# Block orders of the moving reads in a Strassen matmul kernel: 4 words against 16 and 4 by turns, and 512 columns in pieces

## The chip, the cores and the metric

The kernel runs on one core of one Trainium2 chip. The metric is the device time of one execution in microseconds (us); lower is better.

## What is computed

The reference joins an attention block and a two-layer network with softplus. All inputs are float32.

```python
# q, k, v: (8, 8, 576, 64); g_norm: (64,)
kv  = einsum('bhsd,bhse->bhde', k, v)
out = einsum('bhsd,bhde->bhse', q, kv)
rms = sqrt(mean(out * out, axis=-1, keepdims=True) + 1e-06)
x   = (out / rms * g_norm)          # then (B,H,S,D) -> (B*S, H*D) = (4608, 512)
h   = x @ w_in                      # w_in (512, 2048)
g   = maximum(h, 0) + log1p(exp(-abs(h)))
y   = g @ w_out                     # w_out (2048, 512), y (4608, 512)
```

## The kernel before

The precision comes from splitting. Each float32 factor is written as pieces of type float32r (the fast matmul type for 4-byte words), and each product is the sum of three matmuls over `m`, all added up in one PSUM bank.

The work has three phases. In phase 0 the attention part runs (L696 and L720 are its matmuls, L738 and L776 its transposes), and for a first share of the hidden columns the network runs on blocks of 384 tokens: L863 multiplies x by w_in (12 matmuls of 384 columns each time), L870 multiplies the softplus result by w_out (512 columns, three matmuls for each group of 128 tokens).

Phases 1 and 2 take the rest of the hidden columns, in pairs of 128-column chunks and on 512 tokens at a time. They form x times w_in by Strassen's scheme, seven products in place of eight: `wide_step` adds the tasks of one such step. Each product is a call of `product(u, q)`: six matmuls at L1065, `m` from 0 to 2 and in it `kd` from 0 to 1 (two halves of 128 rows of the contraction), all with 256 moving columns, all added up in a quarter of a two-bank PSUM tile that `place(q)` gives. The moving operand is a unit of x (tiles `units`, `early`, `turned`), the stationary one a form of w_in (tiles `pieces`, `w`, `half`). ScalarE and VectorE copy and add between the products (L1107 to L1115), apply softplus, and split the result into `gv` and `g` (L1123, L1126, L1129). Then `mm2(c, i)` multiplies by w_out: three matmuls at L1136, of 512 moving columns each, added up in one PSUM bank for each of four groups of 128 tokens. There the moving operand is `outs[c]`, a tile of `pieces`. In all there are 2,016 matmuls at L1065 and 1,152 at L1136.

The order of the work is not found at run time. A planner (`Plan`) is given each task with a fixed cost and a position, simulates the engines, and writes one static order for each engine's queue, PE's included. Its costs are constants in the code (710 ns for a product, 700 for one `mm2`), so its order does not depend on how an operand is addressed.

The kernel already reads the 256-column operands in an order of its own. `from_the_end` cuts a row into blocks of 4 words and takes the blocks from the last to the first; the words in a block stay in order. Applied to the moving operand and to the PSUM output alike it changes the order in which columns pass, not where they land:

```python
def from_the_end(x):
    return x.rearrange("p (b w) -> p b w", w=4)[:, ::-1]
```

The 512-column matmuls of L1136, and those of L863 and L870, read and write plainly from the first word to the last.

Of the kernel before, what the change touches and what calls it, by code (L numbers as in the profile page):

```python
# [9 lines left out]
F32R = mybir.dt.float32r  # L10
# [8 lines left out]
P = 128  # L19
# [19 lines left out]
    return x.rearrange(f"r ({' '.join(names)}) -> r {' '.join(names)}", **dict(zip(names, shape[1:])))  # L39


def from_the_end(x):

    return x.rearrange("p (b w) -> p b w", w=4)[:, ::-1]


class Slot:
# [159 lines left out]
def kernel(  # L207
# [24 lines left out]
    nc = tc.nc  # L232
# [810 lines left out]
    def wide_step(k):  # L1043
        ph, n, p = STEPS[k]
        ab, gv = slot("ab"), slot("gvp")
        b = starts[k]
# [3 lines left out]
        mine = list(wide_sums)  # L1050
        outs = [w_slots[1, c] for c in (2 * p, 2 * p + 1)]

        def place(q):
            return ab.tile[:, q // 2, q % 2 * HW:(q % 2 + 1) * HW]
# [3 lines left out]
        def product(u, q):  # L1058
            f, i = PRODUCTS[u]
            w = forms[p][f].tile  # L1060
            dst, v = unit_slots[ph, n, u]
            for m in range(3):
                for kd in range(2):
                    at = i * 2 * P + kd * P
                    nc.tensor.matmul(from_the_end(place(q)), lhsT=w[:, m, at:at + P],  # L1065
                                     rhs=from_the_end(dst.tile[:, m, v, kd] if u < 6 else dst.tile[:, m, kd]),
                                     start=(u == 0 and not m and not kd), stop=(m == 2 and kd == 1), skip_group_check=True)

        def multiply(u, q, after, pos, take=(), follows=None):
            f = PRODUCTS[u][0]  # L1070
            give = [unit_slots[ph, n, u][0]] if last else []
            if final and u in (2, 3, 5, 6):
                give.append(forms[p][f])
            return add("PE", 710, lambda: product(u, q), unit_done[ph, n, u] + forms_done[p][f] + list(after), pos, take, give,
                       follows=follows)
# [3 lines left out]
        def gt(dtype=F32):  # L1079
            if dtype not in held:  # L1080
                held[dtype] = sb.tile([P, 2, WIDE], dtype, tag=f"g{gv.place}", name=f"g{gv.place}_{dtype == F32}")
            return held[dtype]

        def gvt(m, dtype=F32):
            y = gv.tile[:, m]
            return y if dtype == F32R else y.bitcast(F32)
# [8 lines left out]
        def begin():  # L1095
            new(ab, None)
            product(0, X)
# [33 lines left out]
        def mm2(c, i):  # L1131
            fresh = first and not c and ph < LAST
            if fresh:
                new(mine[i], [P, d_model])
            for m in range(3):
                nc.tensor.matmul(mine[i].tile, lhsT=(gvt(m, F32R) if m < 2 else gt(F32R))[:, c, i * P:(i + 1) * P], rhs=outs[c].tile[:, m],  # L1136
                                 start=fresh and not m, stop=(last and c == 1 and m == 2), skip_group_check=True)

        seeds = {}
# [19 lines left out]
        for c in range(2):  # L1159
            for i in range(TW):  # L1160
                slot_pos = b + PACE + MM2[TW * c + i]
                a2 = add("PE", 700, lambda c=c, i=i: mm2(c, i),
                         [split_done[c]] + factors_done[1, 2 * p + c] + ([seeds[i]] if i in seeds and not c else []) +
                         ([before[i]] if c or not first else []), slot_pos, [mine[i]] if first and not c and ph < LAST else [], [gv] + ([outs[c]] if final else []))
                before[i] = a2
                if last and c:
                    leave(ph, TW * n + i, mine[i], a2, slot_pos)
# [98 lines left out]
```

## Time and profile before

| | |
|---|---|
| median of 3 runs | 865.46 us (864.7 to 867.28) |
| the profiled execution | 864.34 us, span 862.5 us |
| mean granted TensorE clock | 0.999 |
| PE, PEld busy | 849.7 and 757.7 us (99% and 88%) |
| DVE, ACT busy | 704.6 and 521.2 us (82% and 60%) |
| first L1065 matmul, last matmul start | 338.5 us, 858.4 us |

PE is the matmul unit, PEld its weight loads, which run beside it; DVE is VectorE, ACT is ScalarE. The span goes from the first instruction to the last, the execution's time has some 2 us more around it. The matmuls are pipelined: the duration of one in the trace (282 ns in the mean at L1065, some 390 at L1136) includes the way through the array, and the next starts long before it ends. What counts for the total is the time from one start to the next, and it is read from the start column of the timeline.

### The profile page before, as it was taken

The numbers are of one execution on the slowest core, as the hardware profiler recorded it, in microseconds if no ns is written. First come the engines' busy times: TensorE is split into PE (matmuls) and PEld (weight loads), VectorE is DVE, ScalarE is ACT, GpSimd is POOL, SyncE is SP. The second block draws the span as 40 slices with busy tenths as digits, with TensorE's granted clock in tenths as the row PEclk, the third lists the DMA queues.
The fourth block names the chain that finished last, engine by engine and source line by source line (L and its number), as shares of the span: only waits on it lengthen the run. The fifth ranks groups of instructions, "written<-read, shape, count | busy, mean of one in ns | idle before, by whom it ended". The sixth has DMA issues, their size and how long they took to land.

```text
span 862.5 us, 17080 instructions
## 1 busy us (share of the span) xinstructions
PE 849.7 (99%) x6464; PEld 757.7 (88%) x6464; DVE 704.6 (82%) x995; ACT 521.2 (60%) x980; POOL 76.1 (9%) x79
## 2 busy tenths in 40 slices
PE   8899999999999999999999999999999999999998
PEld 5578888898888999999999999998999899999996
DVE  7988898888788888798888788878788766788873
ACT  6866664436354467766667665654868555566654
POOL 0342223111113300000000000000000000000000
PEclk9999999999999999999999999999999999999999
DMA  9998997779784655436645546645364753778863
GB/s 285 283 234 222 261 263 242 178 235 226 210 188 118 188 157 183 141 107 216 199 158 164 166 154 205 190 158 176 123 196 138 232 165 102 244 234 240 247 187 130
DMA packets 239778, 167.07 MB, mean 194 GB/s; under 512 B 106320, under 2 KB 198736, under 8 KB 239696
## 3 DMA queue, kind: packets, MB, share of 16 engines
q1 hardware_dynamic: 239392, 165.86, 65.7%
q8 instruction: 50, 0.82, 0.4%
q14 instruction: 32, 0.26, 0.1%
q10 hardware_dynamic: 304, 0.13, 0.1%
HBM read 112.98 MB, written 52.95 MB: 192 GB/s over the span
## 4 chain that ended last, share of the span: by engine, by line
PE 94%; DVE 1%; ACT 1%; POOL 0%; issue 0%; ACTq 0%; DVEq 0%
PE banks L1136 30%; PE banks L1065 28%; PE banks L870 16%; PE banks L863 15%; PE banks L720 2%; PE banks L696 2%; PE banks L738 0%; DVE units L643 0%; DVE half L732 0%; PE banks L1230 0%; POOL roots L728 0%; DVE units L646 0%; DVE roots L724 0%; DVE m L464 0%; ACT units L640 0%
## 5 line engine op out<-in xcount | busy, mean ns | idle before, releaser
L1136 PE MATMUL banks<-pieces,gv 128*128 128x512 f32 x768 | 238.0, 391 | 0.0
L1136 PE MATMUL banks<-pieces,g_False 128*128 128x512 f32 x384 | 149.4, 389 | 0.0
L1136 PEld LDWEIGHTS banks<-pieces,gv 128*128 128x128 f32 x768 | 132.5, 188 | 17.3
L863 PE MATMUL banks<-units,pieces 128*128 128x384 f32 x768 | 145.4, 337 | 0.0
L870 PE MATMUL banks<-pieces,gv 128*128 128x512 f32 x576 | 144.9, 396 | 0.0
L863 PEld LDWEIGHTS banks<-units,pieces 128*128 128x128 f32 x768 | 135.5, 188 | 4.9
L870 PEld LDWEIGHTS banks<-pieces,gv 128*128 128x128 f32 x576 | 106.1, 188 | 20.3
L1065 PEld LDWEIGHTS banks<-units,pieces 128*128 128x128 f32 x840 | 112.0, 188 | 6.5 <-ACT banks L1111 0.4
L1065 PE MATMUL banks<-units,pieces 128*128 128x256 f32 x840 | 116.4, 282 | 0.0
L885 ACT ACTIVATE half<-banks 128x384 f32<-128x384 f32 x64 | 31.5, 492 | 97.3 <-PE banks L863 97.1
L1126 DVE TENSOR_TENSOR gv<-g_True,gv 128x1024 fp32r<-128x1024 f32 x47 | 57.5, 1224 | 36.5 <-ACT gv L1123 36.5
L1136 PEld LDWEIGHTS banks<-pieces,g_False 128*128 128x128 f32 x384 | 72.1, 188 | 15.7
L1065 PEld LDWEIGHTS banks<-units,w 128*128 128x128 f32 x504 | 67.3, 188 | 3.7 <-ACT banks L1111 0.2
L1065 PE MATMUL banks<-units,w 128*128 128x256 f32 x504 | 70.3, 282 | 0.0
L728 POOL TENSOR_TENSOR roots<-roots,half 128x8 f32<-128x8 f32 x36 | 62.2, 1727 | 3.0
L1129 DVE SCALAR_TENSOR_TENSOR g_False<-gv 128x1024 fp32r<-128x1024 f32 x47 | 57.6, 1225 | 1.5
L1028 DVE TENSOR_TENSOR units<-loads,units 128x1024 fp32r<-128x1024 f32 x42 | 51.2, 1219 | 6.2 <-ACT units L1025 6.1
L1093 ACT ACTIVATE g_True<-banks 128x256 f32<-128x256 f32 x96 | 36.7, 383 | 31.6 <-PE banks L1065 31.0
L1115 DVE TENSOR_TENSOR g_True<-banks,g_True 128x512 f32<-128x512 f32 x48 | 33.2, 691 | 27.7 <-PE banks L1065 22.5
L930 ACT ACTIVATE m<-banks 128x512 f32<-128x512 f32 x72 | 42.1, 595 | 18.7 <-PE banks L1136 12.8
L1031 DVE SCALAR_TENSOR_TENSOR units<-units 128x1024 fp32r<-128x1024 f32 x42 | 51.4, 1224 | 1.8
L1025 ACT ACTIVATE units<-loads 128x1024 fp32r<-128x1024 f32 x42 | 44.5, 1059 | 12.4 <-PE banks L1065 8.9
(115 smaller groups left out, 1250.2 us busy)
## 6 DMA issues: line engine op xcount, KB each, us to landing
loads<-x SPq DMA_DIRECT2D x180, 128.0 KB, 2.7
part<-m SPq DMA_DIRECT2D x72, 256.0 KB, 2.9
m<-part SPq DMA_DIRECT2D x72, 256.0 KB, 3.3
loads<-form SPq DMA_DIRECT2D x45, 256.0 KB, 3.3
form<-loads SPq DMA_DIRECT2D x36, 256.0 KB, 3.1
raw<-in_moe_w_in_dram SPq DMA_DIRECT2D x16, 512.0 KB, 4.8
loads<-in_k_dram SPq DMA_DIRECT2D x32, 256.0 KB, 4.4
loads<-in_v_dram SPq DMA_DIRECT2D x32, 256.0 KB, 4.6
```

What stands on the lines that cost most here:

```text
L728: nc.gpsimd.tensor_tensor(out=r.tile, in0=r.tile, in1=half, op=ALU.pow)
L863: nc.tensor.matmul(hp, lhsT=w_in.tile[:, i, kd * P:(kd + 1) * P], rhs=xv.tile[:, i, kd], start=(m == 0), stop=(m == 3 * KD - 1))
L870: nc.tensor.matmul(mine[i].tile, lhsT=gv.tile[:, m, i * P:(i + 1) * P], rhs=w_out.tile[:, m], start=(c == cs[0] and m == 0), stop=(c == cs ...
L930: a = add("ACT", 690 if ph == LAST else 600, lambda: nc.scalar.activation(new(ot, [P, d_model]), bank.tile, func=AF.Copy, scale=scale if p ...
L1025: nc.scalar.activation(part_of(0, F32R), xl.tile if m > 1 else xl.tile[:, 0], func=AF.Copy, scale=DOWN)
L1028: nc.vector.tensor_tensor(out=part_of(1, F32R), in0=xl.tile if m > 1 else xl.tile[:, 0], in1=part_of(0), op=ALU.subtract)
L1031: nc.vector.scalar_tensor_tensor(out=part_of(2, F32R), in0=part_of(1), scalar=-RADIX, in1=part_of(0), op0=ALU.mult, op1=ALU.add)
L1065: nc.tensor.matmul(from_the_end(place(q)), lhsT=w[:, m, at:at + P], rhs=from_the_end(dst.tile[:, m, v, kd] if u < 6 else dst.tile[:, m, kd ...
L1093: nc.scalar.activation(dst, src, func=AF.Softplus, scale=1.0 + E)
L1126: nc.vector.tensor_tensor(out=gvt(1, F32R), in0=gt(), in1=gvt(0), op=ALU.subtract)
L1129: nc.vector.scalar_tensor_tensor(out=gt(F32R), in0=gvt(1), scalar=-RADIX, in1=gvt(0), op0=ALU.mult, op1=ALU.add)
L1136: nc.tensor.matmul(mine[i].tile, lhsT=(gvt(m, F32R) if m < 2 else gt(F32R))[:, c, i * P:(i + 1) * P], rhs=outs[c].tile[:, m], start=fresh ...
```

## The change

`from_the_end` takes the block's width. At L1065 the matmuls with kd = 0 read and write in 16 blocks of 16 words, those with kd = 1 in 64 blocks of 4 words as before, both from the last block to the first. At L1136 the 512 columns are read and written in four pieces of 128 words, the last piece first.

```diff
-def from_the_end(x):
+def from_the_end(x, w):
-    return x.rearrange("p (b w) -> p b w", w=4)[:, ::-1]
+    return x.rearrange("p (b w) -> p b w", w=w)[:, ::-1] if w else x
...
-                    nc.tensor.matmul(from_the_end(place(q)), lhsT=w[:, m, at:at + P],
-                                     rhs=from_the_end(dst.tile[:, m, v, kd] if u < 6 else dst.tile[:, m, kd]),
+                    nc.tensor.matmul(from_the_end(place(q), (16, 4)[kd]), lhsT=w[:, m, at:at + P],
+                                     rhs=from_the_end(dst.tile[:, m, v, kd] if u < 6 else dst.tile[:, m, kd], (16, 4)[kd]),
...
-                nc.tensor.matmul(mine[i].tile, lhsT=(gvt(m, F32R) if m < 2 else gt(F32R))[:, c, i * P:(i + 1) * P], rhs=outs[c].tile[:, m],
+                nc.tensor.matmul(from_the_end(mine[i].tile, P), lhsT=(gvt(m, F32R) if m < 2 else gt(F32R))[:, c, i * P:(i + 1) * P],
+                                 rhs=from_the_end(outs[c].tile[:, m], P),
```

`P` is 128.

## The prediction

> **What bounds the kernel now.** I read the page first (busy shares, slices, chain), then the waits of PE, the windows of the Strassen phases, and last the timeline of PE, because nothing but the spacing of matmuls is touched.
>
> ```profile
> PE 849.7 (99%) x6464; PEld 757.7 (88%) x6464; DVE 704.6 (82%) x995; ACT 521.2 (60%) x980; POOL 76.1 (9%) x79
> PEclk9999999999999999999999999999999999999999
> PE 94%; DVE 1%; ACT 1%; POOL 0%; issue 0%; ACTq 0%; DVEq 0%
> PE banks L1136 30%; PE banks L1065 28%; PE banks L870 16%; PE banks L863 15%; PE banks L720 2%; PE banks L696 2%; PE banks L738 0%; DVE units L643 0%; DVE half L732 0%; PE banks L1230 0%; POOL roots L728 0%; DVE units L646 0%; DVE roots L724 0%; DVE m L464 0%; ACT units L640 0%
> ```
>
> The chain is 94% PE, and its two largest lines, 30% and 28%, are the two that change. The clock is granted in full (mean 0.999), so no throttle stands behind any spacing. Next, the windows; the columns are the stretch, its length, then busy time of each engine with its instructions, clock, DMA share and GB/s:
>
> ```profile
> 345.00:400.00 55.00, 55.00 (x340) 49.84 (x338) 46.78 (x63) 37.70 (x73) 0.00 (x0) 1.00 0.50 156
> 400.00:630.00 230.00, 230.00 (x1458) 208.78 (x1457) 192.38 (x235) 145.09 (x272) 0.00 (x0) 1.00 0.53 168
> 630.00:855.00 225.00, 225.00 (x1417) 203.65 (x1416) 169.47 (x189) 136.93 (x243) 0.00 (x0) 1.00 0.63 195
> ```
>
> From 345 to 855 us PE is busy without a gap. The waits of PE in the window from 345 us on give an empty list: no matmul there waits for anybody. So each nanosecond between two matmul starts is in the total, 1 to 1. A busy PE does not tell its rate; the timeline of PE does:
>
> ```profile
> 599.74 0.88 PE L1065 MATMUL banks<-units,w 128*128 128x256 f32 x6
> 600.45 0.62 PE L1136 MATMUL banks<-pieces,gv 128*128 128x512 f32 x2
> 600.90 0.39 PE L1136 MATMUL banks<-pieces,g_False 128*128 128x512 f32 x1
> 601.13 0.62 PE L1136 MATMUL banks<-pieces,gv 128*128 128x512 f32 x2
> 601.58 0.39 PE L1136 MATMUL banks<-pieces,g_False 128*128 128x512 f32 x1
> ...
> 603.17 0.87 PE L1065 MATMUL banks<-units,w 128*128 128x256 f32 x6
> 603.88 0.63 PE L1136 MATMUL banks<-pieces,gv 128*128 128x512 f32 x2
> ```
>
> Read the first column only: six 256-column products take 600.45 - 599.74 = 0.71 us (118 ns each), and the twelve 512-column ones from 600.45 to 603.17 take 2.72 us, 226.7 ns each. The durations in the second column overlap and do not add up.
>
> Over the whole trace, from start to next start: 2,016 matmuls of L1065 mean 118.3 ns and sum 238.5 us; 1,151 of L1136 mean 228.0 and sum 262.5 us. The two lines make 501 of the 862.5 us. The spacing has a fine structure:
> - In L1065 the matmuls with kd = 0 (first, third, fifth of six) take 120.2 ns to the next start, those with kd = 1 take 116.4. Of the 1,008 with kd = 0, 436 stand at 121 to 123 ns and most others at 117 to 119; of those with kd = 1 only 16 are above 120.
> - In L1136 the first of a run behind a product takes 233.1 ns (106 of 166 stand at 235), the second 229.2, the others 226.75.
> - L863 has plain 384-column reads: its settled spacing is 173.3. From 173.3 and 226.7 the slope is 53.4 ns per 128 columns, and 13.3 ns are left per matmul. The same line at 256 columns gives 120 ns, an estimate of what a plain 256-column read would cost; no row has one. The reads by 4 words, last first, are 1.7 ns below it.
>
> **The change part by part.** No instruction is added, removed or moved: the orders of DVE, ACT, POOL and SP are the same, and PE's has the same matmuls, weight loads and semaphores; only the forms differ (kd = 0 becomes 16 blocks of 16 words, kd = 1 stays at 64 blocks of 4, L1136 becomes 4 blocks of 128). Both the moving read and the PSUM write walk in that order, so each product lands where it did. No wait and no DMA is new. The planner's own costs are constants, so its order stays too.
>
> *256 columns, kd = 0.* 1,008 matmuls at 120.2 now. Bounds by the nearest rows: 116.4 (what kd = 1 has), a gain of 1,008 x 3.8 = 3.9 us; and 122.5 (the slow group of kd = 0 for all of them), a loss of 2.3 us. The estimate for a plain read, 120, lies between and changes nothing. I take 118.3: the slow group of 121 to 123 goes, because a matmul no longer follows one with its own stepping, and the usual 118 stays. Gain 1,008 x 1.9 = 1.9 us. This is the choice I am least sure of.
>
> *256 columns, kd = 1.* Its own form stays, its predecessor's changes. It stands at 116.4; the floor seen is 115, the price of falling into the slow group 6 ns each, 1,008 x 6 = 6 us. I take no change: the 16 of 1,008 above 120 say that behind another product it hardly ever falls in it.
>
> *512 columns.* 1,152 at 228.0. The lowest settled value of a 512-column read is 224 (39 of the 576 of L870): a gain of 4 x 1,152 = 4.6 us. The other end is the 233.1 of a first one behind a product: a loss of 5.1 x 1,152 = 5.9 us. I take what the last-first order is worth at 256 columns, 1.7 ns per matmul, for 512 too: 2.0 us.
>
> The rows show that a matmul written in 64 blocks of 4 words runs no slower (118.3) than the line through plain reads gives (120). The Trainium skill, page "PSUM — Partial Sum Buffer", section "Specifications (TRN2)", says that a non-contiguous access pattern slows matmuls significantly; the trace does not bear that out at 4 words. By that rule the 512-column products, plain until now, would become dearer, and the sum would be that of the second rival below.
>
> *What hides behind PE.* If PE gets 1% shorter, DVE is next. In 400 to 630 us it is busy 192.4 of 230; with PE 2 us shorter there, that is 84%. ACT is at 63% and DMA at 53%. The tail behind the last matmul start (858.4 of 862.5 us) is a copy and a store, and is not touched.
>
> *Sum.* 1.9 + 2.0 = 3.9 us off the profiled execution: 864.34 - 3.9 = 860.4 us (span 862.5 to 858.6). The profiled execution lies 1.1 us under the median of the runs, 865.46; against the median it is 861.5 us.
>
> **The rivals.**
>
> *Slow lock at 256 columns, nothing at 512 (no change).* Most starts of L1136 (81%) sit on one phase of a step of 6.67 ns through the whole trace, and spacings move in lumps (227, 231, 235; 116, 118, 122.5). So a form may change the stall inside a matmul without changing where the next can start. Blocks of 16 and of 128 words may then count as plain reads: kd = 0 at 120, 512 columns at 226.7 as before. Price: 1,008 x 0.2 = 0.2 us, so 865.3 us. For it: L863 and L1136 both settle on the same 13.3 ns though their lengths differ. Against it: the 4-word form already leaves that line.
>
> *The pieces slow the 512-column reads (slower).* Place: L1136. Mechanism: three jumps per matmul break the settled phase, and each one runs as the first behind a product does now. Price: 1,152 x (233.1 - 228.0) = 5.9 us, so 871.3 us; if the gain at 256 columns comes as well, 869.4. It decides from a mean of 229.7 ns on, where 1,152 x 1.7 eats the 1.9 us of the 256-column products. For it: L870 shows plain 512-column reads off their phase at 224 to 236 ns by turns, most above 230, and they do not settle within nine matmuls. Against it: 63 jumps per matmul cost L1065 nothing visible. This is also what the page on PSUM, named above as the Trainium skill's, would expect.
>
> *By turns locks the pairs well (faster by more).* kd = 0 reaches 116.4 and the 512-column reads reach 224: 3.9 + 4.6 = 8.5 us, so 857.0 us. For it: both values occur. Against it: 224 occurs only off the settled phase, and is followed by 231 and 236.
>
> *The change does not do what it says:* the forms in the built program are new on each L1065 and L1136 row, so the pattern is in; this rival has no chance worth a number.
>
> **How the numbers follow.** A measurement of this kernel tells about 0.3%, 2.6 us, from no change. Forecast (860 to 863 us) 0.34, more gain (around 857) 0.16, no change 0.13, slower by the 512-column pieces 0.25, slower at 256 columns instead (kd = 0 at 122.5 or kd = 1 drawn into the slow group, 868 to 874 us) 0.12. So faster 0.50, within 0.3% 0.13, slower 0.37. The signs are close, because no row shows these forms: the likeliest case's own range is 859.5 to 863. The range for 8 in 10 goes from 856.8 to 872.
>
> **What would show it.** Start to start in the timeline of the changed kernel: kd = 0 at 117 to 118.5 and its group at 121 to 123 gone; kd = 1 still 116 to 117; L1136 at 225 to 226.5 with the first of a run below 233. Any 512-column mean above 229.7, or a kd = 1 mean above 118.3, makes the prediction wrong. PE must still wait for nobody from 345 us on, and L863 and L870, untouched, must sum to the same 273 us; if they move, something other than the forms is at work.

## The result, and the profile after

The changed kernel takes 866.93 us (median of 22 runs, 865.3 to 869.17), the kernel before 865.27 (22 runs beside it). The ratio is 1.0021, with a 95% interval of 1.0014 to 1.0028: slower by about 1.8 us (0.2%), clear of the noise and small.

From the page of the changed kernel: the span, the busy shares, the chain by engine, and the groups of L1136, L863 and L870. A group's last three columns are its busy time in us, the mean duration of one in ns, and the idle time before it in us.

```profile
span 864.2 us, 17075 instructions
PE 851.1 (98%) x6464; PEld 757.0 (88%) x6464; DVE 704.5 (82%) x995; ACT 521.2 (60%) x980; POOL 76.2 (9%) x79
PE 94%; DVE 2%; ACT 1%; POOL 1%; DMA 1%; issue 1%; SPq 0%; POOLq 0%; DVEq 0%; ACTq 0%
L1136 PE MATMUL banks<-pieces,gv 128*128 128x512 f32 x768 | 239.6, 393 | 0.0
L1136 PE MATMUL banks<-pieces,g_False 128*128 128x512 f32 x384 | 150.9, 393 | 0.0
L863 PE MATMUL banks<-units,pieces 128*128 128x384 f32 x768 | 145.4, 337 | 0.0
L870 PE MATMUL banks<-pieces,gv 128*128 128x512 f32 x576 | 144.9, 396 | 0.0
```

The same groups before, with the largest of L1065:

```profile
L1136 PE MATMUL banks<-pieces,gv 128*128 128x512 f32 x768 | 238.0, 391 | 0.0
L1136 PE MATMUL banks<-pieces,g_False 128*128 128x512 f32 x384 | 149.4, 389 | 0.0
L863 PE MATMUL banks<-units,pieces 128*128 128x384 f32 x768 | 145.4, 337 | 0.0
L870 PE MATMUL banks<-pieces,gv 128*128 128x512 f32 x576 | 144.9, 396 | 0.0
L1065 PE MATMUL banks<-units,pieces 128*128 128x256 f32 x840 | 116.4, 282 | 0.0
```

The untouched lines L863 and L870 have the same busy time and the same mean. A matmul of L1136 has a duration of 393 ns in the mean; before, its two groups had 391 and 389. The groups of L1065 go the other way. After the change they are:

```profile
L1065 PE MATMUL banks<-units,pieces 128*128 128x256 f32 x840 | 115.8, 281 | 0.0
L1065 PE MATMUL banks<-units,w 128*128 128x256 f32 x504 | 69.9, 281 | 0.0
```

PE still waits for nobody from 345 us on (the list is empty). In the windows (columns as in the prediction) it is busy without a gap as before, with fewer matmuls from 400 to 630 us: 1,453 in place of 1,458.

```profile
400.00:630.00 230.00, 230.00 (x1453) 207.59 (x1452) 191.73 (x235) 144.60 (x270) 0.00 (x0) 1.00 0.53 168
630.00:855.00 225.00, 225.00 (x1417) 202.71 (x1417) 170.37 (x190) 137.64 (x245) 0.00 (x0) 1.00 0.63 196
```

Where the time went is seen in the timeline of PE. First the changed kernel, then the kernel before at the same place; the columns are start, duration, instruction and count.

```profile
531.02 0.76 PE L1065 MATMUL banks<-units,pieces 128*128 128x256 f32 x5
531.61 0.63 PE L1136 MATMUL banks<-pieces,gv 128*128 128x512 f32 x2
532.08 0.40 PE L1136 MATMUL banks<-pieces,g_False 128*128 128x512 f32 x1
532.32 0.62 PE L1136 MATMUL banks<-pieces,gv 128*128 128x512 f32 x2
532.77 0.39 PE L1136 MATMUL banks<-pieces,g_False 128*128 128x512 f32 x1
533.00 0.62 PE L1136 MATMUL banks<-pieces,gv 128*128 128x512 f32 x2
```

```profile
530.76 0.63 PE L1136 MATMUL banks<-pieces,gv 128*128 128x512 f32 x2
531.22 0.39 PE L1136 MATMUL banks<-pieces,g_False 128*128 128x512 f32 x1
531.45 0.62 PE L1136 MATMUL banks<-pieces,gv 128*128 128x512 f32 x2
531.90 0.39 PE L1136 MATMUL banks<-pieces,g_False 128*128 128x512 f32 x1
532.13 0.62 PE L1136 MATMUL banks<-pieces,gv 128*128 128x512 f32 x2
```

Take the starts. In the changed kernel the first three matmuls of L1136 last 532.32 - 531.61 = 0.71 us, the next three 533.00 - 532.32 = 0.68. Before, the first three last 531.45 - 530.76 = 0.69 and the next three 0.68. What is new is a start that is longer, in the mean by 17 ns over the runs of L1136 behind a product. There are 165 such runs.

The trace's starts give the balance. "First three" is the mean time that the first three matmuls of a run of L1136 take together, from start to start; three settled ones take 680. The table takes the 165 runs behind a product. Where the text gives the first, second and third matmul one by one, it is the mean over all 166 runs; one run stands behind another line, and its first matmul takes over 310 ns in every kernel, which adds 0.5 ns to the mean of the first.

| kernel | L1065, us | L1136, us | first three, ns |
|---|---|---|---|
| before | 238.5 | 262.5 | 688.7 |
| changed | 236.8 | 265.3 | 705.7 |

So L1065 gains 1.7 us, and L1136 loses 2.9 us, nearly all of it in the first three: 17.0 ns x 165 = 2.8 us. The net loss is 1.1 us. Some 0.5 us more lie ahead of the first matmul of L1065, which starts at 339.0 us in place of 338.5. No changed instruction stands there, and the runs do not show that the change has a part in it.

### The profile page after: what moved, and what is told of

It reads as the page before. It is cut to its first block, busy times and chain, and to the rows that moved or that the text cites. A ratio compares the mean times of both kernels' runs of the same rounds, so it can differ in the third digit from the quotient of the medians.

```text
span 864.2 us, 17075 instructions
## 1 busy us (share of the span) xinstructions
PE 851.1 (98%) x6464; PEld 757.0 (88%) x6464; DVE 704.5 (82%) x995; ACT 521.2 (60%) x980; POOL 76.2 (9%) x79
## 4 chain that ended last, share of the span: by engine, by line
PE 94%; DVE 2%; ACT 1%; POOL 1%; DMA 1%; issue 1%; SPq 0%; POOLq 0%; DVEq 0%; ACTq 0%
PE banks L1136 31%; PE banks L1065 27%; PE banks L870 16%; PE banks L863 15%; PE banks L720 2%; PE banks L696 2%; DMA loads<-in_v_dram 1%; PE banks L1231 0%; PE banks L738 0%; POOL roots L728 0%; DVE half L732 0%; DVE roots L724 0%; PE banks L776 0%; DVE units L643 0%; ACT w L802 0%
## 5 line engine op out<-in xcount | busy, mean ns | idle before, releaser
L1136 PE MATMUL banks<-pieces,gv 128*128 128x512 f32 x768 | 239.6, 393 | 0.0
L1136 PE MATMUL banks<-pieces,g_False 128*128 128x512 f32 x384 | 150.9, 393 | 0.0
L1136 PEld LDWEIGHTS banks<-pieces,gv 128*128 128x128 f32 x768 | 132.6, 188 | 18.6
L863 PE MATMUL banks<-units,pieces 128*128 128x384 f32 x768 | 145.4, 337 | 0.0
L870 PE MATMUL banks<-pieces,gv 128*128 128x512 f32 x576 | 144.9, 396 | 0.0
L863 PEld LDWEIGHTS banks<-units,pieces 128*128 128x128 f32 x768 | 135.5, 188 | 4.8
L870 PEld LDWEIGHTS banks<-pieces,gv 128*128 128x128 f32 x576 | 106.1, 188 | 20.4
L1065 PEld LDWEIGHTS banks<-units,pieces 128*128 128x128 f32 x840 | 111.7, 188 | 7.0 <-ACT banks L1111 0.4
L1065 PE MATMUL banks<-units,pieces 128*128 128x256 f32 x840 | 115.8, 281 | 0.0
L1136 PEld LDWEIGHTS banks<-pieces,g_False 128*128 128x128 f32 x384 | 72.1, 188 | 16.0
L1065 PEld LDWEIGHTS banks<-units,w 128*128 128x128 f32 x504 | 67.1, 188 | 4.0 <-ACT banks L1111 0.2
L1065 PE MATMUL banks<-units,w 128*128 128x256 f32 x504 | 69.9, 281 | 0.0
```

What stands on the lines that cost most here:

```text
L863: nc.tensor.matmul(hp, lhsT=w_in.tile[:, i, kd * P:(kd + 1) * P], rhs=xv.tile[:, i, kd], start=(m == 0), stop=(m == 3 * KD - 1))
L870: nc.tensor.matmul(mine[i].tile, lhsT=gv.tile[:, m, i * P:(i + 1) * P], rhs=w_out.tile[:, m], start=(c == cs[0] and m == 0), stop=(c == cs ...
L1065: nc.tensor.matmul(from_the_end(place(q), (16, 4)[kd]), lhsT=w[:, m, at:at + P], rhs=from_the_end(dst.tile[:, m, v, kd] if u < 6 else dst. ...
L1136: nc.tensor.matmul(from_the_end(mine[i].tile, P), lhsT=(gvt(m, F32R) if m < 2 else gt(F32R))[:, c, i * P:(i + 1) * P], rhs=from_the_end(ou ...
```

## The experiments

Each experiment changes block widths and nothing else, and from the first matmul of L1065 on the sequence of PE's matmuls by line is the same in all the traces; "words" means blocks of that many words, last first. The ratio is to the kernel before, run on the same chip, with its 95% interval. Two theories stood at the outset. A: the pieces of 128 lengthen the first matmuls of L1136. B: the new blocks of L1065 leave PE at a point from which 512-column matmuls start badly, whatever their own order.

| kernel | L1065 (kd = 0, 1) | L1136 | ratio | L1065, us | L1136, us | first three, ns |
|---|---|---|---|---|---|---|
| changed | 16, 4 | 128 | 1.0021 (1.0014 to 1.0028) | 236.8 | 265.3 | 705.7 |
| e1_pieces_only | 4, 4 | 128 | 1.0000 (0.9991 to 1.0008) | 238.5 | 262.4 | 688.6 |
| e2_turns_only | 16, 4 | plain | 1.0032 (1.0020 to 1.0044) | 236.7 | 265.3 | 705.7 |
| e3_plain | plain | plain | 1.0057 (1.0042 to 1.0072) | 240.5 | 264.9 | 697.4 |
| e4_sixteen_both | 16, 16 | plain | 1.0022 (1.0011 to 1.0033) | 238.3 | 263.9 | 686.1 |
| e5_turns_swapped | 4, 16 | plain | 1.0008 (0.9998 to 1.0019) | 236.1 | 265.2 | 694.2 |
| e6_512_w4 | 4, 4 | 4 | 1.0080 (1.0065 to 1.0095) | 239.1 | 268.6 | 699.8 |
| e9_last_pair | 16, 4; last pair 4, 4 | plain | 0.9971 (0.9959 to 0.9982) | 237.7 | 261.2 | 680.9 |
| e10_last_product | 16, 4; last product 4, 4 | plain | 0.9995 (0.9985 to 1.0004) | 237.6 | 262.3 | 687.5 |
| e11_both_ends | 16, 4; first and last pair 4, 4 | plain | 1.0002 (0.9991 to 1.0013) | 238.5 | 262.0 | 685.9 |
| e12_both_ends_pieces | as e11 | 128 | 0.9995 (0.9987 to 1.0004) | 238.5 | 262.0 | 685.9 |

**The two halves of the change, each alone.**

```diff
 # e1_pieces_only, against the changed kernel (L1065 with 4 words)
-from_the_end(place(q), (16, 4)[kd])
+from_the_end(place(q), (4, 4)[kd])
```

> L1136 in four pieces of 128 as changed, L1065 with 4 words everywhere as before. Theory A (the pieces themselves lengthen the first three 512-column matmuls of each run): L1136 mean stays near 230.5 ns and its first three near 235, L1065 stays at 118.3; some 2.9 us above the kernel before, ratio near 1.0033. Theory B (the new 256-column blocks leave PE at a point from which any 512-column read starts badly): L1136 returns to 228.0 with 233, 229 and 227 for the first three, ratio near 1.000.

```diff
 # e2_turns_only, against the changed kernel (L1136 plain)
-from_the_end(mine[i].tile, P)    # and the same for outs[c].tile[:, m]
+from_the_end(mine[i].tile, 0)
```

> L1065 with 16 and 4 words by turns as changed, L1136 plain as before. Theory A: L1065 mean 117.4 ns (1.7 us less than before) and L1136 back at 228.0; ratio near 0.998, faster than both kernels. Theory B: L1065 117.4 and L1136 still near 230.5, ratio near 1.0015.

The groups of L1136 in these two kernels, first the pieces alone, then the turns alone:

```profile
L1136 PE MATMUL banks<-pieces,gv 128*128 128x512 f32 x768 | 238.1, 391 | 0.0
L1136 PE MATMUL banks<-pieces,g_False 128*128 128x512 f32 x384 | 149.5, 389 | 0.0
```

```profile
L1136 PE MATMUL banks<-pieces,gv 128*128 128x512 f32 x768 | 239.7, 394 | 0.0
L1136 PE MATMUL banks<-pieces,g_False 128*128 128x512 f32 x384 | 151.0, 393 | 0.0
```

The pieces alone leave the picture of before (391 and 389; first three 233.1, 229.3, 226.7 ns), and the ratio is 1.0000. The turns alone have all of the changed kernel's loss in matmuls that they do not touch (234.6, 235.8, 235.8). Theory A is refuted, B holds. The half that was meant for L1136 does nothing at all, and the half that gains in L1065 loses more in L1136.

The median with turns alone lies some 3 us above before, its matmuls account for 1.1. Its profile has the first matmul of L1065 at 340.9 us, 2.5 us later than before. The stretch ahead of that has no changed instruction, and it varied from 338.0 to 340.9 us among these profiles. The traces place it: from the first matmul of L863 (44.0 us before, 46.5 here) to the first of L1065 both take 294.5 us, so the whole delay arises in the first 46 us. The granted clock of the first 20 us was 0.83 here and 1.00 before. That is not all of it, for with the pieces alone it was 1.00 too and L863 began at 45.3 us; the cause was not settled.

**What the orders are worth at all.**

```diff
 # e3_plain, against the changed kernel
-(16, 4)[kd] ... P
+(0, 0)[kd] ... 0
```

> Every read plain from the first word on, L1065 and L1136. The line through the settled plain reads of 384 and 512 columns gives 120 ns at 256 columns: L1065 1.7 ns x 2,016 = 3.4 us longer than before, ratio near 1.004. If the block orders do nothing but shift where a matmul starts, L1065 stays near 118.3 and the ratio is near 1.000. L1136 tells beside it how its first matmuls go behind plain products: 233, 229, 227 if what precedes does not matter.

L1065 takes 119.3 ns, behind the first few matmuls of a run 120, where the line through 384 and 512 columns had put it. That line was a good price for a plain 256-column read. L1136 has 2.4 us more than before though it is read as before: again the predecessor's order.

```diff
 # e4_sixteen_both, against the changed kernel (L1136 plain)
-(16, 4)[kd]
+(16, 16)[kd]
```

> L1065 with 16 words for kd = 0 and for kd = 1, last first; L1136 plain. If each form has its own spacing (16 words 118.6, 4 words 116.3), both kd come to 118.6: L1065 mean 118.6, ratio near 1.0005 with L1136 at 228.0. If the taking of turns is what helps, a stream of one form has a slow group again, as the stream of 4 words had (mean 118.3 or more, every second one at 120 or above).

kd = 0 and kd = 1 take 118.1 and 118.4 ns, mean 118.2: a stream of 16 words is no faster than one of 4 (118.3), and neither has what the turns have (117.4). It is the alternation that gains. L1136 did not go back to 228.0 as this expectation had it: it stands at 229.3, because the later matmuls of a run take 229.6 in place of 226.7.

```diff
 # e5_turns_swapped, against the changed kernel (L1136 plain)
-(16, 4)[kd]
+(4, 16)[kd]
```

> Turns the other way round: 4 words for kd = 0, 16 for kd = 1; L1136 plain. If only the taking of turns counts, L1065 stays at 117.4 ns with its two halves exchanged (116.3 and 118.5). If kd itself has a slow half (its addresses), kd = 0 with 4 words is slow again, near 120. Theory B (where the last 256-column matmul ends decides how the 512-column ones begin): the last matmul before L1136 now has 16 words, so its first three change from 234.6, 235.8, 235.8; a theory in which any product of two forms disturbs L1136 leaves them there and the total at 1.003.

The halves exchange: 116.3 ns for kd = 0, 117.9 for kd = 1, mean 117.1. So kd has no slow addresses of its own. L1136 begins with 233.0, 230.7, 230.9 ns and later matmuls of a run stay at 229.5: another last form, another start. The total is not told from before.

**A finer order for the 512-column reads.**

```diff
 # e6_512_w4, against the changed kernel
-(16, 4)[kd] ... P
+(4, 4)[kd] ... 4
```

> L1065 with 4 words everywhere as before, L1136 in 128 blocks of 4 words, last first. Pieces of 128 changed nothing in L1136 (228.0 as plain). If 4 words do at 512 columns what they do at 256 (settled 1.7 ns below the line through plain reads), the settled value drops from 226.7 to about 225 and the ratio is near 0.998. If the rule of the Trainium skill, page PSUM — Partial Sum Buffer, section Specifications (TRN2), on non-contiguous patterns held at 512 columns, L1136 would be dearer. By the rows alone: between 224 and 235, ratio 0.995 to 1.010; I expect 0.998.

A miss: L1136 settles at 233.3 ns in place of 226.7, and the kernel is 0.8% slower. Blocks of 4 words gain at 256 columns (118.3 against 119.3 ns plain) and lose more at 512. The group shows it in the duration, 397 ns for both forms:

```profile
L1136 PE MATMUL banks<-pieces,gv 128*128 128x512 f32 x768 | 242.3, 397 | 0.0
L1136 PE MATMUL banks<-pieces,g_False 128*128 128x512 f32 x384 | 152.3, 397 | 0.0
```

In the same run the slow half of L1065 changed sides, kd = 0 116.8 and kd = 1 120.4, though L1065 is as before. So which half is slow is also set by what stands ahead of the stream; that it is the place where the stream begins is likely, but not shown.

**Mending the start of L1136.** If B holds, only the last two 256-column matmuls ahead of L1136 need to differ. The order of the engines is known when the program is built, so a product can look at its follower.

```diff
 # e9_last_pair, against e2_turns_only
+words = 4 if ahead[0] and m == 2 else (16, 4)[kd]
-from_the_end(place(q), (16, 4)[kd])      # and the same for the moving operand
+from_the_end(place(q), words)
...
+ahead[0] = hasattr(follower.get(id(t)), "wide")     # the next PE task is an mm2
 t.run()
```

> 16 and 4 words by turns, but the last two matmuls of a product that directly precedes L1136 both have 4 words; L1136 plain. Theory B: in the trace of the changed kernel a 4-word matmul that starts where that second-last one starts takes 122.5 ns and the next 116 and ends where the good third of the runs of before began: the first three of L1136 come to 228, 226 and 227 in place of 234.6, 235.8 and 235.8; L1065 costs some 5 ns more for each of the 166 runs (0.9 us). Sum 3.3 us less than with turns alone, 2 us less than before: ratio near 0.9975. If the first three stay at 235 whatever precedes, the ratio is near 1.004.

The first three take 228.1, 226.8 and 226.7 ns; 163 of 165 runs begin well, where none did with turns alone. L1065 pays 0.9 us for it (237.7). The kernel takes 862.54 us against 864.85, ratio 0.9971: faster than the kernel before and the changed one, as forecast to 0.04%. The same place in its timeline (L1138 is `mm2` there):

```profile
529.55 0.62 PE L1138 MATMUL banks<-pieces,gv 128*128 128x512 f32 x2
530.01 0.39 PE L1138 MATMUL banks<-pieces,g_False 128*128 128x512 f32 x1
530.24 0.61 PE L1138 MATMUL banks<-pieces,gv 128*128 128x512 f32 x2
530.69 0.39 PE L1138 MATMUL banks<-pieces,g_False 128*128 128x512 f32 x1
530.91 0.61 PE L1138 MATMUL banks<-pieces,gv 128*128 128x512 f32 x2
```

530.24 - 529.55 = 0.69 and 530.91 - 530.24 = 0.67 us; over all runs the first three take 680.9 ns, as long as settled ones.

```diff
 # e10_last_product, against e9_last_pair
-words = 4 if ahead[0] and m == 2 else (16, 4)[kd]
+words = 4 if ahead[0] else (16, 4)[kd]
```

> 16 and 4 words by turns, but all six matmuls of a product that directly precedes L1136 have 4 words; L1136 plain. Theory B: the product costs some 12 ns more, and the first three of L1136 are at 228, 226 and 227 where the product before it was by turns, and mixed as in the kernel before (235 or 228) where the run is a single product: ratio 0.998 to 1.001. Otherwise near 1.005.

71 of 165 runs begin well (a first matmul under 230 ns), 94 badly; the ratio is 0.9995, as expected. The starts are not mixed, though: what decides is how many products stand together ahead of the run. All 93 runs behind a single product begin badly, and all but one of the 72 behind two or more begin well. In the kernel before, 55 of 165 begin well, and there too the count decides nearly all:

| products ahead | before: good, bad | e10: good, bad | e9: good, bad |
|---|---|---|---|
| 1 | 0, 93 | 0, 93 | 91, 2 |
| 2 | 23, 1 | 24, 0 | 24, 0 |
| 3 | 1, 13 | 13, 1 | 14, 0 |
| 4 | 28, 1 | 29, 0 | 29, 0 |
| 5, 6, 12 | 3, 2 | 5, 0 | 5, 0 |

So a stream of 4 words leaves PE at a bad place after one or three products and at a good one after two or four. The last pair alone at 4 words gives a good place behind any count.

```diff
 # e11_both_ends, against e9_last_pair; e12_both_ends_pieces has P at L1136 besides
-words = 4 if ahead[0] and m == 2 else (16, 4)[kd]
+words = 4 if (ahead[0] and m == 2) or (ahead[1] and m == 0) else (16, 4)[kd]
```

> As with the last pair at 4 words ahead of L1136, and also the first pair of a product that directly follows L1136 at 4 words; all others by turns; L1136 plain. Theory B, read off the traces so far: behind L1136 the turns take 116.6, 119.1, 124.8, 115.1 ns until they settle (475.6), with the first pair at 4 words 117.5, 117, 118, 116 (468.5): some 6 to 7 ns less for each of 166 runs, 1.0 to 1.2 us. L1065 sum near 236.6 us, L1136 stays at 261.2: ratio near 0.996. If a product of both forms must settle anyway, L1065 stays at 237.7 and the ratio at 0.997.

> The same with L1136 in four pieces of 128, last first. If the pieces do nothing for any start (as they did nothing with 4 words in L1065), L1136 has the same 261.2 us and the same first three (228, 227, 227), and the ratio is that of the plain one within 0.1%. If the pieces cost something that the bad starts had hidden, L1136 is above 262.

The first is a miss. The fifth to seventh matmuls behind L1136 take 121.5, 119.6 and 122.4 ns, L1065 is back at 238.5 us and the gain is gone; 74 of 165 runs of L1136 begin well, all 72 behind two or more products but only 2 of the 93 behind a single one, the case in which both ends of one product are changed. I had put the next spacings together from rows of other streams at like starts, and a stream does not go on from a start alone. Of the second the comparison holds: with the pieces of 128, L1136 has the same sum and as many good starts (262.0 us, 74) as without. The 261.2 us of both expectations was not reached.

## Why the prediction failed

By the steps of the prediction:

- *What bounds the kernel.* Right: PE waits for nobody, and the sum of the spacings is the time. L863 and L870 kept their sums (136.7 and 136.1 us before and after).
- *256 columns, kd = 0.* Right in size and in its reason (e4 and e5: it is the alternation that gains): forecast 1.9 us gained, measured 120.2 to 118.6 ns, 1.6 us. The group at 121 to 123 is gone but for 5; 164 matmuls stand at 125 instead, most of them the third behind a run of L1136.
- *256 columns, kd = 1.* Right: 116.4 and 116.3.
- *512 columns.* The step that failed. I took the 1.7 ns that the order of 4 words has at 256 columns, over to pieces of 128 at 512. It was worth 0.0 us (e1, e12), and 4 words at 512 columns would have cost 6.1 us (e6). Without this term the forecast would still have been a gain of 1.9 us.
- *What the sum left out.* The second step that failed, and the one that turned the sign. I costed each line by its own form. No term was there for what the last matmul of L1065 does to the first ones of L1136, though the profile of before showed it: 233.1 and 229.2 ns for the first two of a run, and 55 of 166 that began at 227 or 228. I had used these rows as a price for the pieces and not asked what made a run begin well or badly. The term is +2.9 us, against 1.7 us that L1065 gained.
- *The rivals.* The slower one, from a mean of 229.7 ns on, had the place (L1136 at 230.5) and the wrong mechanism: not three jumps per matmul, but the predecessor. My own test, a mean above 229.7, came out against the forecast. The faster one was right that pairs lock (233.3 ns once settled), but L1136 did not reach 224. The rival with no change, 865.3 us, is off by 1.6 us, and for the wrong reason: a gain and a loss nearly cancel. That 866.93 us lies within the stated range is luck too; the range was wide enough for the slower rivals, and none of them has the mechanism.

Why a run begins badly is shown so far: it goes with the place of its first start on a step of 6.67 ns. The settled spacings are whole numbers of this step: 173.3 ns is 26, 226.7 is 34, 233.3 is 35. For the six kernels before, changed, e1, e2, e9 and e10, in all of which the last matmul ahead of L1136 has 4 words, I counted the place of each first start in sixteenths of the step, from where the settled matmuls of L1136 within 20 us of it start. (The trace gives starts to 1 ns, some two sixteenths.) Of 343 starts at 12 to 15 sixteenths all but one took 226 to 229 ns; of 637 at 0 to 4 all but two took 233 to 236; ten lie between. The form is the same, only the place differs. In e11 and e12, also with 4 words last, 148 starts at 13 to 15 took 227 or 228 ns, and the other 182 stand at 7 to 9 and took 232 or 233. Behind 16 words (e4, e5) no place is as good (230 to 234).

With turns each settled pair of matmuls takes about 233.3 ns, 35 steps, so further products do not move the place; in the changed kernel all 165 runs begin at 1 to 3 sixteenths, a bad place. What in the hardware has this step was not found out.

The Trainium skill, page "PSUM — Partial Sum Buffer", section "Specifications (TRN2)", says that non-contiguous patterns slow matmuls significantly. By these runs that is so for 4 words at 512 columns (233.3 against 226.7 ns), not for pieces of 128 (228.0 in both), and the other way for 4 words at 256 columns (118.3 against 119.3 plain). Each form changes the moving read and the PSUM write together, so no run here shows which of the two costs the time.

## What to carry to other kernels

When PE waits for nobody, cost a change of a matmul's form by start to start, and ask of each matmul type also how it begins behind its new predecessor; the switch between types is a term of its own. Look at the spread of a spacing, not at its mean alone: two groups in one row can mean that something outside the row chooses between them, here the number of products ahead and the form of the last ones. A gain in one line that is lost at its border can be had by giving only the matmuls at the border another form.

## What the runs showed of the hardware that was not expected

Matmuls of float32r on operands of the same size and line have several spacings, most between 224 and 236 ns at 512 columns and between 115 and 125 at 256. For the first 512-column matmul behind 4-word ones the choice goes with the start's place on a step of 6.67 ns. With 4 words throughout, that place goes by the number of products ahead: 0 of 93 runs begin well behind one product, 23 of 24 behind two. Two forms by turns lock into pairs of 233.3 ns; a stream of either form alone has pairs of 236.5 ns in the mean. Reading order alone moved the kernel by 1.1%, from 0.9971 to 1.0080 of the time before.
